# Three units of quarter products in the first matrix product of each token group instead of two, with their weight sums kept in DRAM

## The chip, the cores and the metric

The kernel runs on one core of a Trainium2 chip. Its engines are PE (TensorE: matmuls, with a weight load for each), DVE (VectorE), ACT (ScalarE), POOL (GpSimd) and SP (SyncE, which here only issues DMAs); each has its own queue and works it off in order. The metric is the device time of one execution in microseconds, as the median of several runs. One execution is also recorded by the hardware profiler; all durations below come from that one.

## The reference, cut to what matters

```python
# attention: q, k, v are (8, 8, 576, 64), fp32
scores = np.matmul(q, k.transpose(0, 1, 3, 2)) / 8
thresh = np.max(scores, axis=-1, keepdims=True) - tau
scores = np.where(scores >= thresh, scores, -1e9)
attn = np.exp(scores - np.max(scores, axis=-1, keepdims=True))
attn = attn / (attn.sum(axis=-1, keepdims=True) + 1e-9)
x = merge_heads(np.matmul(attn, v))            # (8, 576, 512)
# feed-forward: w_ch1 is (512, 2048), w_ch2 is (2048, 512)
mu, var = x.mean(-1), x.var(-1)
xn = (x - mu) / np.sqrt(var + 1e-6) * g_ln
out = x + np.maximum(xn @ w_ch1, 0) @ w_ch2
```

## The kernel before, in words

**Slots and groups.** The attention part runs over 72 slots, 9 per batch element (slot n belongs to element b = n // 9, with s = n % 9). A slot handles four blocks of 128 queries against 576 keys. The feed-forward part runs over 16 groups of 288 tokens, two per element. Its matmuls are poured into the slots by a generator (`ffn_steps`), step by step, as quotas allow (`second_part`, `dealt`, `owed`); the order on each engine is the order of issue. A group becomes ready some slots after its attention: an even group starts in the slot with s = 7, an odd group in the slot with s = 2 of the next element. Each of these groups fills about four and a half slots.

**One slot.** PE computes the scores (L434) into two PSUM tiles, `sc[0]` and `sc[1]`, three banks each. DVE reduces them to row maxima (`neg`, L450), POOL forms the threshold (`thr`, L454), ACT takes the exponentials (L463) into the room `e`, DVE masks and sums them (L473), POOL divides by the sums (L490), DVE transposes blocks of 32 (L559), SP writes the result to DRAM (`scr`, L580) and reads it back in the next slot as `em` and `er` (L594, L599). PE multiplies by the values one slot later (L638, and L649 at the end of the slot, into a corner of the score tiles). There is one room `e`: the exponentials of a slot overwrite it and so wait for the write of the slot before. In slots with s = 8, 0, 1, 2 DVE also transposes the next pair's q and k (`turn`, L368 to L378) between `neg` and the masking, after POOL has scaled q (L350); SP then loads the pair after that (L120).

**First part of a group.** hidden = relu(w_ch1 x), 16 chunks of 128 hidden features by 288 tokens. A plain chunk is 4 products (each two matmuls of 64 columns of weights, `product`, L103) over 288 tokens. A *unit* computes four chunks at once by a scheme of seven quarter products of 144 tokens instead of eight, with sums of weights and of x: one running PSUM tile `chain`, one tile `p2`, two regions in `sc[0]`, four additions on DVE (L940) and six ACT operations (L934 to L974). `chain`, `p2`, a plain chunk's `p1` and the segments of the second part share two PSUM banks (`ps_ff`), each free again when it has been copied out. The first unit of a group writes `chain` twice before the score tile; a later one writes `chain`, `p2` and then `sc[0]`, which must by then have been masked:

```python
order = (p5, p6, p3, p7) if k else (p6, p5, p7, p3)
```

Groups 0 and 1 are all plain. From group 2 on, two units are used, chunks 0 to 3 and 12 to 15, in two following slots; chunks 4 to 11 are plain.

**The sums of w_ch1.** While group 1 runs its second part (slots 13 to 15), `sums_of_w1` forms the weight sums: for each unit four steps, each three operations of 128x128 on DVE and one on POOL. One of the four is written over w_ch1 itself; the others, 12 pieces of 128x128 a unit, stay in SBUF: 21 in `extra`, two at the end of the room `e1`, one in the place of `ident`.

**Second part of a group.** Seven segments of quarter products of w_ch2 (`segment`), each 32 matmuls of 144 columns, with four sums of `hidden` formed in place (t3, t2, t4, t1, L1125, by_fours: two operations of 128x576 each). Those are queued in `drops` and issued by `drip`, or by `need` when due. b11 and b12 are the early and late tokens of chunks 0 to 7, b21 and b22 those of chunks 8 to 15. Segments in order: b11 (y11), b21, b12 after t3 = b22 - b12, b11 after t2 = b11 + t3 (y12), b21 after t4, b11 after t1, b22.

**Tail.** After slot 71 the last two groups run without attention beside them.

Of the kernel before, what the change touches and what calls it, by code (L numbers as in the profile page):

```python
# [18 lines left out]
def kernel(  # L19
# [824 lines left out]
                    eng.tensor_tensor(out=out[at], in0=a[at], in1=b[at], op=op)  # L844
                    yield

    UNITS = (((0, 1), (2, 3)), ((12, 13), (14, 15)))
    PLAIN = [d for d in range(ND) if all(d not in t for u in UNITS for t in u)]
    sums_due = []
    last_added = set()  # L850
# [2 lines left out]
        n, i = divmod(ready(g), QUARTERS)  # L853
        return [n + (i > 0) + k for k in range(len(UNITS))]

    def piece_of(k, which, c, m):


        i = ((k * 3 + which) * 2 + c) * 2 + m
        if i < 21:  # L860
            return extra[:, i]
        if i < 23:
            at = NB * 128 - 256 + (i - 21) * 128
            return flat(e_room[1])[:, at : at + 128]
        return ident

    def sums_of_w1():


        for k, (f1, f2) in enumerate(UNITS):  # L870
            for c in range(2):
                for m in range(2):
                    cols = [slice(128 * t[m], 128 * t[m] + 128) for t in (f1, f2)]
                    a11, a12 = (w1_sb[2 * j + c][:, cols[0]] for j in range(2))
                    a21, a22 = (w1_sb[2 * j + c][:, cols[1]] for j in range(2))
                    p2, p3, p4 = (piece_of(k, i, c, m) for i in range(3))
                    for eng, out, a, b, op in (
                        (nc.vector, p3, a11, a21, ALU.subtract),
                        (nc.vector, a21, a21, a22, ALU.add),
                        (nc.vector, p2, a21, a11, ALU.subtract),  # L880
                        (nc.gpsimd, p4, a12, p2, ALU.subtract),
                    ):
                        eng.tensor_tensor(out=out, in0=a, in1=b, op=op)
                    yield

    sums_of_x = {}

# [18 lines left out]
    def unit(g, xc, k):  # L906


        f1, f2 = UNITS[k]
        t1, t2, t3, t4 = sums_of_x[g]  # L910
        of = lambda f, j: hidden[:, f[0] : f[0] + 2, (early, late)[j]]
        h11, h12, h21, h22 = of(f1, 0), of(f1, 1), of(f2, 0), of(f2, 1)
        w_of = lambda f, j: lambda c, m: w1_sb[2 * j + c][:, 128 * f[m] : 128 * f[m] + 128]
        s_of = lambda which: lambda c, m: piece_of(k, which, c, m)
        x_of = lambda i, j: lambda c: xc[:, 2 * i + c, (early, late)[j]]
        t_of = lambda t: lambda c: t[:, c]
        other = [
            sc[0][:, 512 * i : 512 * i + TOK].rearrange("p (m t) -> p m t", m=2) for i in range(2)
        ]

        def steps(bank, lhs, rhs, first, last):
            for c in range(2):
                for m in range(2):
                    product(
                        bank[:, m], lhsT=lhs(c, m), rhs=rhs(c),
                        start=first and c == m == 0, stop=last and c == m == 1,
                        skip_group_check=True,
                    )
                    yield c == m == 1

        chain = ps_ff.tile([128, 2, HT], F32, tag="ff", name="chain")
        for _ in steps(chain, w_of(f1, 0), x_of(0, 0), True, False):
            yield 3, 0.5
        nc.scalar.copy(h12, chain)  # L934
        p2 = ps_ff.tile([128, 2, HT], F32, tag="ff", name="p2")
        for _ in steps(p2, w_of(f1, 1), x_of(1, 0), True, True):
            yield 3, 0.5

        def add(out, a, b):
            ins = nc.vector.tensor_tensor(out=out, in0=a, in1=b, op=ALU.add)  # L940
            if any(a is t for t in other):
                other_reads.append(ins.ins)

        def after_p6():
            nc.scalar.copy(h22, chain)
            sums_due.append(lambda: add(h12, other[0], h22))

        def after_p7():
            nc.scalar.copy(h21, chain)
            sums_due.append(lambda: add(h22, other[0], h21))  # L950

        sums_due.append(lambda: add(h11, p2, h12))
        p5 = steps(other[0], w_of(f2, 0), t_of(t1), True, True), lambda: None
        p6 = steps(chain, s_of(0), t_of(t2), False, False), after_p6
        p7 = steps(chain, s_of(1), t_of(t3), False, False), after_p7
        p3 = (
            steps(other[1], s_of(2), x_of(1, 1), True, True),
            lambda: sums_due.append(lambda: add(h12, other[1], h12)),
        )
        order = (p5, p6, p3, p7) if k else (p6, p5, p7, p3)  # L960
        for i, (part_of, after) in enumerate(order):
            for end in part_of:
                if end:
                    after()
                stop = end and now < QUARTERS * NS and (i == 3 or i == 0 and part < 2)
                yield 4 if stop else 3, 0.5
        for end in steps(chain, w_of(f2, 1), t_of(t4), False, True):
            if not end:
                yield 3, 0.5
        run_all(sums_due)  # L970
        nc.scalar.activation(h21, chain, func=AF.Relu)
        both = hidden[:, f1[0] : f1[0] + 2]
        nc.scalar.activation(both, both, func=AF.Relu)
        nc.scalar.activation(h22, h22, func=AF.Relu)  # L974
        yield 2 if k else 3, 0.5
# [10 lines left out]
    def add_squares(sq, *which):  # L986
        for c in which:
            nc.gpsimd.tensor_tensor(out=sq[:, 0], in0=sq[:, 0], in1=sq[:, c], op=ALU.add)  # L988

    def first_units(g):  # L990


        xc = centred[g]
        plain, slots = PLAIN[:], unit_slots(g)
        sq = hidden[:, ND - NK :]
        k = 0
        due = False
        while plain or k < len(UNITS):
            if k < len(UNITS) and (not plain or now // QUARTERS >= slots[k] and part > 1):
                yield from unit(g, xc, k)  # L1000
                k += 1
                if k == 1:
                    due = plain and owed >= 1
                    if not due:
                        bank = ps_ff.tile([128, HT], F32, tag="ff", name="var")
                        rb = variance(g, average(spare[g], bank, sq[:, 0], True, eps_sb))
                        yield 2, 0.5
                continue
            d = plain.pop(0)
            bank = ps_ff.tile([128, 512], F32, tag="ff", name="p1")  # L1010
            p1 = bank[:, :TOK]
            for c in range(NK):
                if due and c == NK - 1:
                    spread = average(spare[g], bank[:, TOK : TOK + HT], sq[:, 0], False, eps_sb)
                    yield 1, 0.5
                product(
                    p1, lhsT=w1_sb[c][:, d * 128 : (d + 1) * 128], rhs=xc[:, c],
                    start=(c == 0), stop=(c == NK - 1),
                )
                if c < NK - 1:  # L1020
                    yield 1, 1
            nc.scalar.activation(hidden[:, d], p1, func=AF.Relu)  # L1022
            if due:
                due = False
                rb = variance(g, spread)
            yield 2, 1
        sums_of_x.pop(g)
        return rb

    def first_part(g):  # L1030
# [64 lines left out]
    def second_quarters(g, rb):  # L1095
# [83 lines left out]

        dve, pool = nc.vector, nc.gpsimd  # L1180
        ends_here = g == NG - 1
        later(("t3", 3, by_fours, pool, b12, b22, b12, ALU.subtract), urgent=pool)
        banks_taken[0] = True
        yield from segment(w2[0, 0], b11, y11)
        need("t3")
        later(("t2", 3, by_fours, dve, b11, b11, b12, ALU.add), urgent=dve)
        yield 2, 0.5
        p2 = yield from segment(w2[0, 1], b21)
        need("t2")
        later(("t4", 3, by_fours, pool, b21, b21, b11, ALU.subtract), urgent=pool)  # L1190
# [42 lines left out]
    def ffn_steps(g):  # L1233
        rb = yield from (first_part if g < 2 else first_units)(g)
        sums = sums_of_w1() if g == 1 else iter(())
        for i, step in enumerate((second_quarters if g else second_plain)(g, rb)):
            if i % 13 == 12:
                next(sums, None)
            yield step

# [31 lines left out]
    def second_part(n, i):  # L1272
# [13 lines left out]
        else:  # L1286
            if i == 0:
                share = remain / (ready(g + 1) // QUARTERS - n)
                if has_unit:
                    first = [(share - UNIT_COST) * r / sum(ROOM[:2]) for r in ROOM[:2]]  # L1290
                    dealt[:] = [*first, UNIT_COST - 2, 2]
                else:
                    dealt[:] = [share * r / sum(ROOM) for r in ROOM]
            owed += dealt[i]
# [4 lines left out]
        steps = 0  # L1299
        whole = i in (0, QUARTERS - 1) or i == 1 and has_unit  # L1300
        got = 1 if i in (0, QUARTERS - 1) else 3 if i == 2 and has_unit else 2
        least = 2 if has_unit and i < 2 else 0.5
        while queue and (owed >= least or got == 3 or got == 1 and whole):
            got, cost = next(queue[0], (None, 0))
            if got is None:
# [228 lines left out]
```

## Time and profile before

| | |
|---|---|
| Median of 3 runs | 1316.91 us (1315.94 to 1317.62) |
| The profiled execution's own time | 1317.26 us |
| Its span | 1315.4 us |
| PE busy | 1280.6 us |
| DVE / POOL / ACT busy | 948.3 / 638.2 / 515.0 us |
| Granted TensorE clock | 0.997 |
| DMA | 214.11 MB, mean 163 GB/s |
| Share of SP's DMA queue, of 16 engines | 54.8% |

In a timeline, each line is a group of like instructions: start and duration in us, engine, line of the kernel, operation, output <- inputs, shape, number of records, and in brackets the idle time of the engine before it with what ended it. The table of waits gives, for a waiting instruction and the one that released it, the total in us, the number of times and the longest. "+8.03" in the text means 8.03 us after the first score matmul of that slot. Slots quoted: slot 38 starts at 640.68, 39 at 657.91, 44 at 739.08, 45 at 757.92 and 46 at 774.38 us.

### The profile page before, as it was taken

Reading aid. Unit: us, or ns where it says so; the run is one execution under the profiler, and the core shown is the slowest. Engines: PE = TensorE matmul, PEld = TensorE weight load, DVE = VectorE, ACT = ScalarE, POOL = GpSimd, SP = SyncE. Lnnn points to the kernel's source line nnn. Section 1 sums busy time; section 2 is a strip of 40 time slices with the busy share of each in tenths; the row PEclk is TensorE's granted clock in tenths of the full one; section 3 lists DMA queues with packets and bytes.
Section 4 is the critical chain, followed back from the end, with each engine's and each line's share of the span. In section 5 each row is a group of like instructions: output and inputs, shape, how many; then the busy total and the mean of one; then the engine's idle time right before and its main releaser. Section 6 shows DMA issues by size and latency. Waiting matters only on the chain.

```text
span 1315.4 us, 43423 instructions
## 1 busy us (share of the span) xinstructions
PE 1280.6 (97%) x18648; PEld 1050.7 (80%) x18648; DVE 948.3 (72%) x1722; ACT 515.0 (39%) x1163; POOL 638.2 (49%) x858
## 2 busy tenths in 40 slices
PE   8899889999999999999999999999999999999997
PEld 7665556879788887978879897888878788798977
DVE  7879878976777587776868777775877768687223
ACT  5866343343433434242343424334342423434130
POOL 3465565545445354544535454453545445354413
PEclk9999999999999999999999999999999999999999
DMA  8937865466644675546744566446764457453111
GB/s 154 295 112 185 205 171 193 151 173 171 191 164 163 170 205 168 166 159 155 216 154 158 172 169 192 163 163 171 190 191 157 160 146 202 157 168 140 52 19 19
DMA packets 335311, 214.11 MB, mean 163 GB/s; under 512 B 247376, under 2 KB 292688, under 8 KB 327056
## 3 DMA queue, kind: packets, MB, share of 16 engines
q1 hardware_dynamic: 329008, 210.46, 54.8%
q8 instruction: 146, 2.39, 0.7%
q10 hardware_dynamic: 5952, 0.74, 0.4%
q14 instruction: 45, 0.37, 0.1%
q0 software_dynamic: 160, 0.15, 0.1%
HBM read 124.00 MB, written 87.29 MB: 161 GB/s over the span
## 4 chain that ended last, share of the span: by engine, by line
PE 74%; DVE 3%; POOL 1%; DMA 1%; ACT 1%; issue 1%; POOLq 0%; DVEq 0%; ACTq 0%
PE seg L103 28%; PE p L103 16%; PE chain L103 8%; PE sc L434 8%; PE sc L638 7%; PE sc L103 4%; PE sc L649 2%; DVE e L473 1%; DMA scr<-e 1%; DVE neg L450 1%; POOL sum L692 0%; DVE e L559 0%; POOL thr L454 0%; PE mean L708 0%; POOL e L490 0%
## 5 line engine op out<-in xcount | busy, mean ns | idle before, releaser
L103 PE MATMUL p<-xc,w 128*64 128x288 f32 (+1 forms) x2752 | 327.9, 389 | 4.9 <-ACT hidden L1022 2.9
L450 DVE TENSOR_REDUCE neg<-sc 128x2 f32<-128x1152 f32 x144 | 189.5, 1353 | 144.7 <-PE sc L434 142.6
L103 PEld LDWEIGHTS p<-xc,w 128*64 128x64 f32 x2752 | 188.0, 137 | 123.9 <-issue 11.2
L490 POOL TENSOR_SCALAR e<-e,den 128x576 f32<-128x576 f32 x264 | 205.4, 791 | 95.2 <-DVE den L478 94.9
L103 PE MATMUL seg<-hidden,w 128*64 128x144 f32 x3840 | 244.0, 287 | 0.0
L103 PEld LDWEIGHTS seg<-hidden,w 128*64 128x64 f32 x3840 | 234.8, 137 | 9.3 <-issue 7.9
L473 DVE SCALAR_TENSOR_TENSOR e<-sc,thr,e 128x576 f32<-128x576 f32 x288 | 222.3, 809 | 15.6 <-POOL thr L454 8.6
L454 POOL TENSOR_SCALAR thr<-neg,low_sb 128x2 f32<-128x2 f32 x144 | 45.4, 316 | 335.8 <-DVE neg L450 334.5
L463 ACT ACTIVATE e<-sc,neg 128x576 f32<-128x576 f32 x288 | 196.5, 752 | 17.3 <-DMA scr<-e 13.5
L559 DVE STREAM_TRANSPOSE e<-e 128x1152 f32<-128x1152 f32 (+1 forms) x113 | 163.8, 1451 | 22.7 <-POOL e L490 22.0
L434 PE MATMUL sc<-kT,qT 64*64 64x384 f32 (+3 forms) x2048 | 139.4, 403 | 1.6 <-DVE e L473 1.6
L638 PE MATMUL sc<-em,v_in 128*64 128x128 f32 (+1 forms) x2368 | 130.6, 264 | 3.7 <-DVE e L473 2.0
L638 PEld LDWEIGHTS sc<-em,v_in 128*64 128x64 f32 x2368 | 122.3, 138 | 7.1 <-DVE e L473 3.0
L103 PE MATMUL seg<-hidden,stage 128*64 128x144 f32 x1920 | 124.3, 286 | 0.6 <-ACT y L1140 0.6
L103 PEld LDWEIGHTS seg<-hidden,stage 128*64 128x64 f32 x1920 | 117.4, 137 | 3.6 <-issue 2.5
L434 PEld LDWEIGHTS sc<-kT,qT 64*64 64x64 f32 x2048 | 76.0, 133 | 42.6 <-issue 21.3
L1140 ACT COPY part<-seg 128x288 f32<-128x288 f32 x74 | 29.9, 404 | 181.3 <-PE seg L103 152.9
L1125 POOL TENSOR_TENSOR hidden<-hidden 128x576 f32<-128x576 f32 x60 | 84.2, 1423 | 30.0 <-ACT hidden L1022 16.8
L663 ACT COPY x<-sc 128x128 f32<-128x128 f32 x120 | 31.2, 265 | 164.8 <-PE sc L434 109.1
L1125 DVE TENSOR_TENSOR hidden<-hidden 128x576 f32<-128x576 f32 x60 | 52.6, 905 | 41.7 <-PE seg L103 35.8
L988 POOL TENSOR_TENSOR hidden<-hidden 128x288 f32<-128x288 f32 x48 | 39.0, 812 | 77.9 <-ACT hidden L1335 76.4
L1022 ACT ACTIVATE hidden<-p 128x288 f32<-128x288 f32 x112 | 47.2, 422 | 56.0 <-PE p L103 55.9
(163 smaller groups left out, 1633.9 us busy)
## 6 DMA issues: line engine op xcount, KB each, us to landing
scr<-e SPq DMA_DIRECT2D x60, 1152.0 KB, 5.0
em<-scr SPq DMA_DIRECT2D x63, 1024.0 KB, 5.7
out_dram<-ot SPq DMA_DIRECT2D x248, 36.0 KB, 3.7
q_in<-in_q_dram SPq DMA_DIRECT2D x120, 72.0 KB, 2.6
er<-scr SPq DMA_DIRECT2D x132, 64.0 KB, 5.1
k_in<-in_k_dram SPq DMA_DIRECT2D x116, 72.0 KB, 2.9
v_in<-in_v_dram SPq DMA_DIRECT2D x28, 256.0 KB, 5.5
w<-in_moe_w_ch_dram SPq DMA_DIRECT2D x10, 512.0 KB, 8.6
```

The source lines that it names most:

```text
L103: nc.tensor.matmul(out[r], lhsT=lhsT[:, r], rhs=rhs, **flags)
L434: mm = nc.tensor.matmul(sc[h][64 * i : 64 * i + 64, at : at + n], lhsT=ql[r] if s == HP else qT[r, half, j * 128 + 64 * i : j * 128 + 64 * ...
L450: nc.vector.tensor_reduce(out=neg[:, i], in_=pairs[h], axis=AXL.X, op=ALU.max, negate=True,)
L454: nc.gpsimd.tensor_scalar(out=thr[:, i], in0=neg[:, i], scalar1=-1.0, scalar2=low_sb, op0=ALU.mult, op1=ALU.add,)
L463: nc.scalar.activation(blocks_of(es, i, n), like(blocks[i], n), func=AF.Exp, bias=neg[:, i : i + 1])
L473: nc.vector.scalar_tensor_tensor(out=e, in0=like(blocks[i], n), scalar=thr[:, i : i + 1], in1=e, op0=ALU.is_ge, op1=ALU.mult, accum_out=de ...
L490: nc.gpsimd.tensor_scalar(out=e, in0=e, scalar1=den[:, i : i + 1], scalar2=1.0, op0=ALU.mult, op1=ALU.mult,)
L559: nc.vector.transpose(et[:, :, at], et[:, :, at])
L638: mm = nc.tensor.matmul(dst[64 * h : 64 * h + 64], lhsT=vt[:, h, c, :], rhs=pick(em[:, 2 * j : 2 * j + 2, c], h), start=c == 0 and first, ...
L988: nc.gpsimd.tensor_tensor(out=sq[:, 0], in0=sq[:, 0], in1=sq[:, c], op=ALU.add)
L1022: nc.scalar.activation(hidden[:, d], p1, func=AF.Relu)
L1125: eng.tensor_tensor(out=out[at], in0=in0[at], in1=in1[at], op=op)
```

## The change

A third unit takes chunks 4 to 7; chunks 8 to 11 remain plain. The twelve pieces of each unit's sums are stored to DRAM (`sums0` to `sums2`, 768 KB each). In SBUF there are two rooms of twelve pieces: 12 of `extra`, and the other 9 of `extra` with the end of `e1` and the place of `ident`. Units use the rooms in turn (`room_for`); when a unit has been issued, the sums of the unit after next are loaded into its room on SP, at quarter 1 of the slot after (`unit_and_load`, `load_sums`). The third unit runs inside the second part, between the segment y11 and the segment on b21; a slot with one of the first two units has two plain chunks ahead of it. From group 2 on, t3 and t2 are issued after the third unit, and both run on POOL. The third unit's sums pass through tiles of the pool `o` on their way to DRAM. The steps of `sums_of_w1` come every 9 steps instead of every 13, twelve of them.

```diff
-    UNITS = (((0, 1), (2, 3)), ((12, 13), (14, 15)))
+    UNITS = (((0, 1), (2, 3)), ((4, 5), (6, 7)), ((12, 13), (14, 15)))
...
+    PIECES = 12
+    stored = [
+        dram.tile([128, PIECES, 128], F32, tag=f"sums{k}", bufs=1, name=f"sums{k}")
+        for k in range(len(UNITS))
+    ]
+    def rooms_of(room):
+        if room == 0:
+            return [(0, extra[:, :PIECES])]
+        end = flat(e_room[1])[:, NB * 128 - 256 : NB * 128]
+        return [
+            (0, extra[:, PIECES:21]),
+            (9, end.rearrange("p (i c) -> p i c", c=128)),
+            (11, ident.rearrange("p (i c) -> p i c", i=1)),
+        ]
+    def room_for(g, k):
+        return (len(UNITS) * g + k) % 2
+    def store_sums(k):
+        for at, pieces in rooms_of(room_for(2, k)):
+            nc.sync.dma_start(out=stored[k][:, at : at + pieces.shape[1]], in_=pieces)
+    def load_sums(g, k):
+        for at, pieces in rooms_of(room_for(g, k)):
+            nc.sync.dma_start(out=pieces, in_=stored[k][:, at : at + pieces.shape[1]])
...
     def sums_of_w1():
...
-                    p2, p3, p4 = (piece_of(k, i, c, m) for i in range(3))
+                    if k < 2:
+                        p2, p3, p4 = (piece_of(room_for(2, k), i, c, m) for i in range(3))
+                    else:
+                        two = [ffn.tile([128, TOK], F32, tag="o", bufs=4, name="sum") for _ in range(2)]
+                        p2, p3, p4 = two[0][:, :128], two[0][:, 128:256], two[1][:, :128]
...
+                    for i, piece in enumerate((p2, p3, p4) if k == 2 else ()):
+                        nc.sync.dma_start(out=stored[k][:, (i * 2 + c) * 2 + m], in_=piece)
                     yield
+            if k < 2:
+                store_sums(k)
...
+    def second_half(g, k):
+        n = unit_slots(g)[k]
+        while now < QUARTERS * min(NS, n + 1) and (now < QUARTERS * n or part < 2):
+            yield 0, 0
+    def unit_and_load(g, k):
+        yield from second_half(g, k)
+        n = max(now // QUARTERS, unit_slots(g)[k])
+        yield from unit(g, centred[g], k)
+        h, i = divmod(len(UNITS) * g + k + 2, len(UNITS))
+        if h < NG:
+            at_quarter(max(n, now // QUARTERS) + 1, 1, load_sums, h, i)
     def first_units(g):
...
+        for k in range(2):
+            for d in PLAIN[2 * k : 2 * k + 2]:
...
+            yield from unit_and_load(g, k)
...
-        later(("t3", 3, by_fours, pool, b12, b22, b12, ALU.subtract), urgent=pool)
-        banks_taken[0] = True
+        t3 = "t3", 3, by_fours, pool, b12, b22, b12, ALU.subtract
+        t2 = "t2", 3, by_fours, dve if g == 1 else pool, b11, b11, b12, ALU.add
+        if g == 1:
+            later(t3, urgent=pool)
+            banks_taken[0] = True
         yield from segment(w2[0, 0], b11, y11)
-        need("t3")
-        later(("t2", 3, by_fours, dve, b11, b11, b12, ALU.add), urgent=dve)
+        if g == 1:
+            need("t3")
+            later(t2, urgent=dve)
         yield 2, 0.5
+        if g > 1:
+            yield from unit_and_load(g, 2)
+            sums_of_x.pop(g)
+            later(t3, t2, urgent=pool)
+            banks_taken[0] = True
         p2 = yield from segment(w2[0, 1], b21)
...
-            if i % 13 == 12:
+            if i % 9 == 8:
                 next(sums, None)
...
-                if has_unit:
-                    first = [(share - UNIT_COST) * r / sum(ROOM[:2]) for r in ROOM[:2]]
-                    dealt[:] = [*first, UNIT_COST - 2, 2]
+                if has_unit and n < unit_slots(g)[2]:
+                    dealt[:] = [4, 4, UNIT_COST - 2, 2]
+                elif has_unit:
+                    dealt[:] = [3, 5, UNIT_COST - 2, max(2, share - 6 - UNIT_COST)]
...
-        least = 2 if has_unit and i < 2 else 0.5
+        least = 2 if has_unit and i < 2 and n < unit_slots(g)[2] else 0.5
```

More of the change, by code (lines that the diff above doesn't have):

```diff
@@ L854, in unit_slots, with piece_of @@
         return [n + (i > 0) + k for k in range(len(UNITS))]
[L856 to L865, printed above, removed]
+    PIECES = 12
[12 more added lines that the diff above has]
+        ]
+    def piece_of(room, which, c, m):
+        i = (which * 2 + c) * 2 + m
+        at, pieces = [r for r in rooms_of(room) if r[0] <= i][-1]
+        return pieces[:, i - at]
+    def room_for(g, k):
[6 more added lines that the diff above has]
+            nc.sync.dma_start(out=pieces, in_=stored[k][:, at : at + pieces.shape[1]])
     def sums_of_w1():
@@ L913, in unit @@
         w_of = lambda f, j: lambda c, m: w1_sb[2 * j + c][:, 128 * f[m] : 128 * f[m] + 128]
-        s_of = lambda which: lambda c, m: piece_of(k, which, c, m)
+        s_of = lambda which: lambda c, m: piece_of(room_for(g, k), which, c, m)
         x_of = lambda i, j: lambda c: xc[:, 2 * i + c, (early, late)[j]]
@@ L990, in first_units @@
     def first_units(g):
         xc = centred[g]
-        plain, slots = PLAIN[:], unit_slots(g)
         sq = hidden[:, ND - NK :]
-        k = 0
         due = False
[L998 to L1026, printed above, removed]
@@ L1027, in first_units @@
-        sums_of_x.pop(g)
+        for k in range(2):
+            for d in PLAIN[2 * k : 2 * k + 2]:
+                bank = ps_ff.tile([128, 512], F32, tag="ff", name="p1")
+                p1 = bank[:, :TOK]
+                for c in range(NK):
+                    if due and c == NK - 1:
+                        spread = average(spare[g], bank[:, TOK : TOK + HT], sq[:, 0], False, eps_sb)
+                        yield 1, 0.5
+                    product(
+                        p1, lhsT=w1_sb[c][:, d * 128 : (d + 1) * 128], rhs=xc[:, c],
+                        start=(c == 0), stop=(c == NK - 1),
+                    )
+                    if c < NK - 1:
+                        yield 1, 1
+                nc.scalar.activation(hidden[:, d], p1, func=AF.Relu)
+                if due:
+                    due = False
+                    rb = variance(g, spread)
+                yield 2, 1
+            yield from unit_and_load(g, k)
+            if k == 0:
+                due = now >= QUARTERS * NS
+                if not due:
+                    bank = ps_ff.tile([128, HT], F32, tag="ff", name="var")
+                    rb = variance(g, average(spare[g], bank, sq[:, 0], True, eps_sb))
+                    yield 2, 0.5
```

## The prediction

> **What bounds the kernel now.** I read the page first: its span, then the busy shares.
>
> ```profile
> span 1315.4 us, 43423 instructions
> PE 1280.6 (97%) x18648; PEld 1050.7 (80%) x18648; DVE 948.3 (72%) x1722; ACT 515.0 (39%) x1163; POOL 638.2 (49%) x858
> ```
>
> PE is the bound, with 34.8 us of idle time in the whole span. The second view, the waits of PE alone between 220 and 1180 us (columns: total us, times, longest), shows that almost none of that idle time lies in the periodic part:
>
> ```profile
> PE p L103 <- ACT hidden L1022: 2.9, 7, 1.4
> PE sc L103 <- DVE e L473: 0.9, 6, 0.2
> PE seg L103 <- ACT y L1140: 0.6, 2, 0.4
> ```
>
> So a microsecond taken from PE is a microsecond gained as long as no new wait arises, and every new wait of PE is lost in full. The third view is the timeline of PE in slots 43 and 44 (start, duration, instruction group). Each matmul of the program leaves two records here.
>
> ```profile
> 722.05 7.98 PE L103 MATMUL p<-xc,w 128*64 128x288 f32 x64
> 729.86 1.15 PE L103 MATMUL chain<-xc,w 128*64 128x144 f32 x16
> ...
> 735.74 1.92 PE L638 MATMUL sc<-em,v_in 128*64 128x128 f32 x32
> 737.49 1.15 PE L103 MATMUL chain<-t,w 128*64 128x144 f32 x16
> 738.47 0.41 PE L708 MATMUL var<-hidden,avg_sb 128*64 128x144 f32 x4
> ```
>
> Four plain chunks of the first part (64 records of 288 columns) last from 722.05 to 729.86, 7.81 us. A unit (112 records of 144 columns) lasts from 729.86 to 738.47 without the values from 735.74 to 737.49, 6.86 us. A record of 144 columns costs 61 ns and one of 288 costs 122 ns: halving the columns halves the time.
>
> **Term 1, the matmuls.** Chunks 4 to 7 go from plain to a unit in each of 14 groups: 14 x (7.81 - 6.86) = **-13.3 us**. The built program agrees in count: 9,662 matmuls instead of 9,326, which is 14 x (56 - 32) more, of half the width. [...]
>
> **Term 2, waits that go.** In slot 39 (an odd group's second unit behind a single plain chunk) the timeline has PE idle for 0.25 us before p2 (an eviction on ACT queued behind exponentials) and 0.15 us before the first product into the score banks. With two plain chunks ahead, as in slot 38, neither shows. Six groups (3, 5, ... 13): 6 x 0.40 = **-2.4 us**. The 1.4 us in the table is slot 16 and belongs to term 4.
>
> **Term 3, waits that come in the even groups.** Units now begin behind two chunks, 5.98 us after the slot's scores begin (slot 38: 640.68 to 646.66). For the second and third unit the first product into the score banks comes third, 2 x 1.02 us later, at +8.03. It must wait until DVE has masked both blocks of sc0. In slot 44 DVE turns the next pair's q and k first:
>
> ```profile
> 741.24 2.82 DVE L450 TENSOR_REDUCE neg<-sc 128x2 f32<-128x1152 f32 x2 [2.38 <-PE sc L434]
> 743.97 0.77 DVE L368 STREAM_TRANSPOSE kT<-k_in 128x576 f32<-128x576 f32 x1
> 745.19 0.77 DVE L372 STREAM_TRANSPOSE qT<-q_in 128x256 f32<-128x256 f32 x2 [0.45 <-POOL q_in L350]
> ...
> 747.45 0.08 DVE L473 DVE_READ_ACCUMULATOR e<-sc,thr,e 128x1 f32 x1
> ```
>
> Scores began at 739.08, the second block ends at 747.53 (+8.45), and a release takes 0.05 (slot 39: 664.65 to 664.70): PE waits 8.50 - 8.03 = 0.47 us. Before, the unit stood behind three chunks and waited for nothing. In slot 45, now also a unit's slot with a turn, t3 no longer stands ahead of the scaling of q on POOL, so slot 46's row holds (turn done at +6.74), then two blocks of together 1.53 us (slot 38), +0.05: +8.32, 0.29 us of wait.
> Slot 45 has a second candidate. The sums of the third unit (768 KB) are loaded on SP behind slot 44's q and k (issued until +11.7) and ahead of that slot's write of weights (issued at +13.3, landed at +18.7 by the next fetch's issue, 757.82). Slot 44 becomes 18.84 - 3.9 + 0.47 = 15.4 us long, so the landing, +3.3 in slot 45, lies 0.4 us ahead of the exponentials (+3.71) that overwrite the same room. The load adds between nothing and 2.0 us (768 KB at about 390 GB/s: the windows give 412 and 370 in the two microseconds from 740). Behind the exponentials, on ACT, stands the copy of y11 that frees p2's bank; it ended at +6.64 against +7.0 needed, 0.36 us of cover. So slot 45 costs 0.3 to 1.25 us; I take 0.5, because q's and k's small packets still fill the engines while the load starts and only part of it falls on the write. Per group about 1.0, in the six even groups 2 to 12 (group 14 has no turn): **+6 us**, bounds 4.6 and 10.3. Odd groups stay clear: their turn falls on the first unit (needed at +9.0, ready at +8.3), their other two slots have no turn (ready at +6.75).
>
> **Term 4, the start.** The sums of w_ch1 grow from 8 steps to 12 (two subtractions and an addition on DVE, one subtraction on POOL each), still within slots 13 to 15, where DVE has no idle time left from 229.55 until 265.2:
>
> ```profile
> 229.55 2.62 DVE L450 TENSOR_REDUCE neg<-sc 128x2 f32<-128x1152 f32 x2 [0.95 <-PE sc L434]
> ...
> 262.59 2.61 DVE L450 TENSOR_REDUCE neg<-sc 128x2 f32<-128x1152 f32 x2
> 265.60 0.82 DVE L473 SCALAR_TENSOR_TENSOR e<-sc,thr,e 128x576 f32<-128x576 f32 x1 [0.40 <-POOL thr L454]
> ```
>
> The 8 steps took 11.7 us of the DVE timeline, 1.46 each (0.86 where POOL rests, 1.7 or more where it works). Four more are 5.8 us; 0.95 of idle time takes its part, so slot 16's neg comes 4.9 us later. That slot's evictions, behind the exponentials, already cost PE 1.42 us; now p2 starts at 267.43 + 4.9 and ends at 273.3, where before the same work, two chunks (3.9 us) less than at 271.76, was done at 267.85. Loss **+5.5 us**. Bounds 3.1 (0.86 a step) and 7.1 (1.6 a step, and 1 us for the third unit's sums, whose tiles are reused only when their stores have landed: DVE waits there, and the weights' transposes, xc and neg are queued behind it).
>
> **Term 5, the tail.** Without attention between them, the last two chain stretches of a unit wait for the copy (0.50 us before 1279.90, in the last group's second unit). One such unit becomes three, and a plain eviction behind the variance can cost 0.5; the 0.46 and 0.18 us of waits around the old variance go: **+0.9 us**, 0.4 to 1.4.
>
> **At nothing**, with the cover: t2 moves from DVE to POOL (1.423 us instead of 0.905, 28 instructions, 40 us of POOL): it is due one segment of 3.9 us after t3, and it ends about 5.9 us after the unit, ahead of y12's segment at 7.8. In slot 41 it holds thr back by 1.4 us; the values that need those weights come 2 us after them. If that cover went, 1 us in 7 groups. DVE keeps its sum: four additions a unit (1.8 us) for two t2 (1.8 us). ACT gets six operations of 2.72 us for four of 1.69; it is 39% busy, and the order of evictions that could hurt is in term 3. The other loads land a slot or more ahead of use; 33 MB beside 214 MB lie on queues at 55%.
>
> **Sum.** -13.3 - 2.4 + 6.0 + 5.5 + 0.9 = -3.3 us on the profiled execution's own 1317.26 us: 1314.0. That execution stands 0.35 above the median of 1316.91: **1313.6 us**. With the bounds: -7.6 to +3.1, so 1309.3 to 1320.0.
>
> **Rivals.** (a) The waits don't come: DVE's extra steps find POOL at rest and the score banks are ready; only 3.1 of the start and 2 of term 3 stay. -13.3 - 2.4 + 5.1 + 0.4 = -10.2, about 1306.7. Against it: the rows above are already at their limit. Chance 0.15.
> (b) Slower: the loads in front of the weights' write. One mechanism, in slot 45 of six groups: if the 768 KB move nearer to the page's mean of 163 GB/s (4.8 us) than to 390, the write lands about 3 us later, at +6.3, the exponentials start 2.6 us late, and PE waits 2.2 us for p2's bank instead of 0.5: 6 x 1.7 = 10 us more, about 1324. It decides from a landing at +4.3 in slot 45, where the gain is gone (0.55 us more, six times). For it: the write already delays exponentials in the waits of ACT (13.5 us, 11 times between 220 and 1180 us). Against it: the engines moved 412 GB/s in the microsecond from 740. Chance 0.2.
> (c) The change does not do what it says: excluded by the counts of the built program; the order of PE shows all three units in every group from 2 on. Chance below 0.01.
>
> **How the numbers follow.** The forecast has 0.65. A measurement of this kernel can tell about 0.2%, 2.6 us, from no change: faster means below 1314.3, slower above 1319.5. The forecast's own range lies with 0.6 of its chance below 1314.3 and with 0.05 above 1319.5. Faster: 0.39 + 0.15 = 0.54. Slower: 0.2 + 0.03 = 0.23. Same: 0.23. The range reaches into both rivals: 1306 to 1322.5.
>
> **What would show it.** Right: matmuls p of 288 columns from 2304 records to 1408; PE waiting for DVE e L473 about 0.5 us in slot 44 and again in slot 45; slot 16's neg about 5 us later than 262.59; slot 40 at 15.3 us instead of 13.7. Wrong: PE waits in slots 38 to 42, a wait of PE for the loaded sums, exponentials waiting for the write by over 1 us in slot 45, or units longer than 6.9 us.

## The result, and the profile after

The changed kernel takes 1337.57 us (median of 4 runs, 1331.73 to 1338.7); the kernel before takes 1317.26 us (4 runs, 1315.94 to 1318.7). The ratio is 1.0145, 95% interval 1.0114 to 1.0176. The forecast was 1313.6 us, with a range of 1306 to 1322.5: wrong in sign and outside the range.

The head of the page of the changed kernel:

```profile
span 1336.1 us, 45057 instructions
PE 1280.0 (96%) x19320; PEld 1090.4 (82%) x19320; DVE 961.8 (72%) x1762; ACT 528.6 (40%) x1191; POOL 674.2 (50%) x890
...
PE 66%; DMA 4%; DVE 3%; ACT 2%; POOL 2%; issue 2%; POOLq 0%; ACTq 0%; DVEq 0%; SPq 0%
```

PE's busy time should have fallen by 13.3 us and fell by 0.6; the span grew by 20.7. Part of the missing fall is matmuls at half speed (below), which count as busy: with the load moved (first experiment) PE is busy for 1275.1 us. The last line is the chain that ended last: DMA holds 4% of the path (before: 1%), nearly all of it the write of the weights.

The waits of PE between 220 and 1180 us (total us, times, longest), 4.4 us before:

```profile
PE p L103 <- ACT y L1181: 13.9, 6, 3.1
PE chain L103 <- ACT hidden L1057: 2.6, 1, 2.6
PE p L103 <- DVE xc L742: 2.4, 1, 2.4
PE sc L638 <- DVE e L473: 2.2, 3, 1.3
PE sc L103 <- DVE e L473: 1.9, 6, 0.3
```

The first line is one wait in each of the six even groups: the third unit's p2 waits for the bank that y11's copy frees. The next three lines are the start (slots 14 to 16). The last line is the wait for the masked score bank that the prediction put at 0.29 and 0.47 us.

Where the 20.7 us lie follows from the starts of the slots in the two traces. The row on the start counts slots 14 to 16 against a slot 16 that is 3.78 us shorter, as the first unit's slot is in every other even group (15.30 instead of 19.08 us).

| Part of the run | Predicted | Measured |
|---|---|---|
| Slots 0 to 13 | 0 | +0.6 |
| Start, slots 14 to 16 | +5.5 | +9.6 |
| Six even groups (2 to 12) | 6 x (-0.95 + 1.0) = +0.3 | +20.7 |
| Six odd groups (3 to 13) | 6 x (-0.95 - 0.40) = -8.1 | -10.1 |
| Slot 70 and the tail, groups 14 and 15 | 2 x -0.95 + 0.9 = -1.0 | -0.2 |
| Sum (of the rounded rows) | -3.3 | +20.6 |

The 20.7 us of the even groups lie almost wholly in one slot of each, the slot of the third unit (18, 27, 36, 45, 54, 63). With the load moved (first experiment below) this slot lasts 21.51 us; here it lasts 23.43, 21.72, 25.55, 26.15, 25.68 and 25.90, together 19.4 us more. Slot 45, which starts at 763.28, on three engines. SP from slot 44 on, ACT, and then PE:

```profile
760.13 0.62 SPq L891 DMA_DIRECT2D extra<-sums  x1
761.02 0.36 SPq L580 DMA_DIRECT2D scr<-e  x1
...
770.58 0.38 SPq L594 DMA_DIRECT2D em<-scr  x1
```

```profile
770.61 2.64 ACT L463 ACTIVATE e<-sc,neg 128x576 f32<-128x576 f32 x4 [3.51 <-DMA scr<-e]
773.12 0.42 ACT L1181 COPY y<-seg 128x288 f32<-128x288 f32 x1
```

```profile
769.30 1.15 PE L103 MATMUL chain<-xc,w 128*64 128x144 f32 x16
773.58 1.96 PE L103 MATMUL p<-xc,w 128*64 128x144 f32 x16 [3.13 <-ACT y L1181]
775.33 2.11 PE L103 MATMUL sc<-t,w 128*64 128x144 f32 x16
777.25 1.17 PE L103 MATMUL chain<-t,extra 128*64 128x144 f32 x16
```

The same places in the kernel before (SP in slot 44, ACT in slot 45, which starts at 757.92):

```profile
752.40 0.36 SPq L580 DMA_DIRECT2D scr<-e  x1
...
757.82 0.38 SPq L594 DMA_DIRECT2D em<-scr  x1
```

```profile
761.63 2.64 ACT L463 ACTIVATE e<-sc,neg 128x576 f32<-128x576 f32 x4
764.16 0.40 ACT L1140 COPY y<-seg 128x288 f32<-128x288 f32 x1
```

The third unit's sums are loaded 0.9 us ahead of the write. The fetch that waits for the write goes out 9.56 us after it (5.42 in the same slot before), at +7.30 of slot 45. The exponentials that overwrite the room start at +7.33 instead of +3.71. Behind them on ACT stands y11's copy (773.12, though its segment had ended at 769.47), and behind that PE's p2: 3.13 us of wait. This is one of the prediction's own signs of being wrong: the exponentials wait 3.51 us for the write, and 1 us was its limit. Then PE pays a second time: 16 records of 144 columns take 1.96 and 2.11 us instead of 1.15 to 1.20. This is the granted clock: 0.91 in the 20 us from 760, where the kernel before has 1.00 in every such stretch from 160 to 1300 us.

### The profile page after: what moved, and what is told of

The parts are those of the page before. It is cut to its first block, busy times and chain, and to the rows that moved or that the text cites. A ratio compares the mean times of both kernels' runs of the same rounds, so it can differ in the third digit from the quotient of the medians.

```text
span 1336.1 us, 45057 instructions
## 1 busy us (share of the span) xinstructions
PE 1280.0 (96%) x19320; PEld 1090.4 (82%) x19320; DVE 961.8 (72%) x1762; ACT 528.6 (40%) x1191; POOL 674.2 (50%) x890
## 4 chain that ended last, share of the span: by engine, by line
PE 66%; DMA 4%; DVE 3%; ACT 2%; POOL 2%; issue 2%; POOLq 0%; ACTq 0%; DVEq 0%; SPq 0%
PE seg L103 27%; PE chain L103 10%; PE p L103 8%; PE sc L434 7%; PE sc L638 7%; PE sc L103 5%; DMA scr<-e 4%; DVE e L473 2%; ACT e L463 1%; PE sc L649 1%; DVE neg L450 1%; POOL e L490 1%; DMA v_in<-in_v_dram 1%; POOL q_in L350 0%; POOL sum L692 0%
## 5 line engine op out<-in xcount | busy, mean ns | idle before, releaser
L103 PE MATMUL p<-xc,w 128*64 128x288 f32 (+1 forms) x2080 | 233.4, 374 | 18.8 <-ACT y L1181 13.9
L103 PEld LDWEIGHTS p<-xc,w 128*64 128x64 f32 x2080 | 139.4, 138 | 100.2 <-ACT y L1181 15.5
L463 ACT ACTIVATE e<-sc,neg 128x576 f32<-128x576 f32 x288 | 196.4, 754 | 22.2 <-DMA scr<-e 17.9
L1166 POOL TENSOR_TENSOR hidden<-hidden 128x576 f32<-128x576 f32 x88 | 122.6, 1419 | 97.4 <-ACT hidden L1008 88.6
L454 POOL TENSOR_SCALAR thr<-neg,low_sb 128x2 f32<-128x2 f32 x144 | 39.7, 276 | 252.8 <-DVE neg L450 250.8
L103 PE MATMUL chain<-t,extra 128*64 128x144 f32 x1344 | 99.2, 291 | 0.0
L103 PEld LDWEIGHTS chain<-t,extra 128*64 128x64 f32 x1344 | 86.8, 140 | 0.0
```

Of the source, the lines that this page charges most:

```text
L103: nc.tensor.matmul(out[r], lhsT=lhsT[:, r], rhs=rhs, **flags)
L454: nc.gpsimd.tensor_scalar(out=thr[:, i], in0=neg[:, i], scalar1=-1.0, scalar2=low_sb, op0=ALU.mult, op1=ALU.add,)
L463: nc.scalar.activation(blocks_of(es, i, n), like(blocks[i], n), func=AF.Exp, bias=neg[:, i : i + 1])
L1166: eng.tensor_tensor(out=out[at], in0=in0[at], in1=in1[at], op=op)
```

## The experiments

All times are medians, beside runs of the kernel before on the same chip (1318.2 to 1318.7 us in these series). Theory A: the 768 KB load ahead of the weights' write, in a slot 44 that has become 3.2 us shorter, is the loss of the even groups. Rivals: the shorter slot alone (theory B); the 31 MB of extra traffic as such (theory C); the order on SP alone.

**The load behind the write.**

```diff
-            at_quarter(max(n, now // QUARTERS) + 1, 1, load_sums, h, i)
+            at = 3 if k == 0 and g % 2 == 0 else 1
+            at_quarter(max(n, now // QUARTERS) + 1, at, load_sums, h, i)
```

> The 768 KB load of the third unit's sums in the even groups is issued on SP behind the weights' write of the same slot instead of ahead of it; nothing else changes. Theory A (the load ahead of the write is the whole loss): the write lands 5 to 6 us after its issue instead of 9.5, the exponentials of slot 45 wait under 1 us, slot 45 lasts 21.1 to 21.7 us instead of 26.15, and the sum over the six even groups, 20.4 us, is gone: 1317 us, 1315 to 1319. Theory B (slot 44 is 3.2 us shorter than before, so the next exponentials come too early for any write): PE still waits over 1.5 us in slot 45 and the time stays above 1328.

1319.17 us (10 runs); ratio to before 1.0008 (0.9998 to 1.0019) instead of 1.0145: about 18 us are back. The same place in the trace, slot 45 starting at 759.52, and the line of ACT's waits between 220 and 1180 us (17.9 us in 8 before the edit):

```profile
757.25 0.36 SPq L580 DMA_DIRECT2D scr<-e  x1
757.65 0.43 SPq L891 DMA_DIRECT2D extra<-sums  x1
...
764.06 0.38 SPq L594 DMA_DIRECT2D em<-scr  x1
```

```profile
ACT e L463 <- DMA scr<-e: 3.1, 4, 1.3
```

The write is issued at the same place, +13.31 of slot 44, and has landed 6.81 us later, the worst of the six. Five third-unit slots last 21.50 or 21.51 us, this one 21.72. The load itself is still there and still arrives in time. The shorter slot alone is therefore not the cause.

**No loads of sums at all.**

```diff
-            at_quarter(max(n, now // QUARTERS) + 1, 1, load_sums, h, i)
+            pass
```

> All loads of stored sums are left out, so units 2 and 3 multiply by whatever lies in their room (the output is not the reference's; the work of PE, DVE, ACT and POOL is the same). Theory A: as with the load behind the write, 1315 to 1317.5, within 2 us of it. Theory C (31 MB more of transfers cost something in every slot): well below that run, 1305 to 1312.

1318.24 us (10 runs), ratio 0.9997 (0.9988 to 1.0006). That is 0.9 us less than with the load behind the write, no more than the scatter of the runs. The loads elsewhere, and the traffic as such, cost about a microsecond at most: theory C falls. Nor does PE's table of waits in the changed kernel show any wait for loaded sums.

**Half of the load ahead.**

```diff
+            if k == 0 and g % 2 == 0:
+                at_quarter(n, 1, load_half, h, i, 0)
+                at_quarter(n, 3, load_half, h, i, 1)
```

> Half of that load (384 KB) stays ahead of the weights' write, the other half goes behind it. Theory A, if the delay goes by bytes: the write lands 7 to 7.5 us after its issue, PE waits about 1 us in slot 45, too short to lower the clock; slot 45 lasts 22 to 23 us, the time is 1320 to 1327. If a transfer ahead of the write costs by its place and not by its bytes, 1333 or more.

1321.24 us (6 runs), ratio 1.0029 (1.0017 to 1.0041). PE waits 0.74 us in slot 36 and 1.14 in slot 45, nothing in the other four. That a wait of about 1 us would leave the clock up was the author's estimate; the changed kernel's trace has waits of 0.38 us (slot 27) and 2.09 us (slot 18) with the granted clock at 1.00 after both. On average the delay grows faster than the bytes, as the table below shows: the mean goes from 5.7 to 6.6 to 8.7 us for 0, 384 and 768 KB ahead, though single slots overlap.

**The kernel before with the same load ahead.** The first unit's sums are read once more from DRAM, in the even groups' second slot, between k and the write.

```diff
+    def load_again():
+        nc.sync.dma_start(out=extra[:, :12], in_=stored)
...
+                if k == 0 and g % 2 == 0:
+                    at_quarter(max(now // QUARTERS, slots[0]) + 1, 1, load_again)
```

> The kernel before with one more load: after the even groups' first unit its 768 KB of sums are read again from DRAM into the same room, issued on SP in slot 44 between the k load and the weights' write, where the third unit's load stood. Theory A with the shorter slot: the load delays the write by 3 to 4 us here too, but slot 44 is 18.84 us long, so the write (issued at +13.3, landed some 9 us later, +3.5 to +4 of slot 45) meets the exponentials at +3.7 and costs PE nothing or a few tenths: 1317 to 1320. If a load ahead of the write costs by itself, whatever the slot's length: 1325 to 1340.

1317.86 us (10 runs), ratio 0.9996 (0.9985 to 1.0006): no loss. The slowest of its writes, in slot 35 (SP, then ACT in slot 36, which starts at 606.50):

```profile
600.38 0.62 SPq L870 DMA_DIRECT2D extra<-sums  x1
601.10 0.36 SPq L580 DMA_DIRECT2D scr<-e  x1
610.79 0.38 SPq L594 DMA_DIRECT2D em<-scr  x1
```

```profile
610.82 2.64 ACT L463 ACTIVATE e<-sc,neg 128x576 f32<-128x576 f32 x4 [0.51 <-DMA scr<-e]
613.33 0.42 ACT L1149 COPY y<-seg 128x288 f32<-128x288 f32 x1
```

This write is as late as in the changed kernel, 9.69 us after its issue, but the slot is 18.84 us long: it lands at +4.29 instead of +7.30. y11's copy ends at 613.75, +7.25, and PE, which has two segments (8.06 us) behind its scores here, asks for that bank only at 616.44, +9.94. In the changed kernel the third unit asks at 770.45, +7.17. So the load was harmless alone, and the shorter slot was harmless alone; together with the earlier need for the bank they cost 19 us. That the earlier need has a part is worked out from the times, not run: here a request at +7.17 would have waited 0.1 us, and in the changed kernel, where y11's copy ends at +10.26, a request at +9.94 would have waited 0.3 us instead of 3.13.

**The load ahead, but early.** Quarter 0 of slot 44 instead of 1.

```diff
+            at = 0 if k == 0 and g % 2 == 0 else 1
+            at_quarter(max(n, now // QUARTERS) + 1, at, load_sums, h, i)
```

> The changed kernel with the even groups' third load issued early in slot 44 (behind the fetch of the turned weights, ahead of the stores and the loads of q and k, some 8 us earlier than in the changed kernel), so it still stands ahead of the weights' write on SP. Theory A (the two transfers share the engines when they are in flight together): the load has landed before the write is issued at +13.3, the write lands within 5 to 7 us, slot 45 lasts 21.5 us: 1317 to 1321. If it is the order on SP that delays the write: as the changed kernel, above 1330.

1319.43 us (10 runs), ratio 1.0002 (0.9987 to 1.0016). The load is still ahead of the write on SP, and the write lands in 5.2 to 6.4 us. So the order on SP alone did not delay it. Nor did a load in flight beside it: in the first experiment the load goes out 0.4 us after the write, and the write still lands in 5.7 us on average. The write was late where all of the load stood ahead of it with its bytes still to move (issued 0.7 to 1.6 us earlier in the changed kernel): 8.7 us on average there, 8.5 in the kernel before with the same load. One slot of six lost 1.6 us, where the write itself was issued at +15.17: it stands on SP behind the loads of q and k, and the last q load went out at +12.09 (+9.24 in the changed kernel). SP's waits between 740 and 757 us put 1.9 us on the fetch `em` and 0.3 on the early load.

From the issue of the write to the issue of the fetch that waits for it, in us, in the six slots before the third unit's (the same slots in the kernel before):

| Kernel | 17 | 26 | 35 | 44 | 53 | 62 | mean |
|---|---|---|---|---|---|---|---|
| before | 5.38 | 5.11 | 5.18 | 5.42 | 6.74 | 5.79 | 5.6 |
| changed | 8.53 | 6.78 | 9.14 | 9.56 | 9.10 | 9.20 | 8.7 |
| load behind | 5.47 | 4.95 | 6.11 | 6.81 | 5.41 | 5.35 | 5.7 |
| no loads | 5.43 | 6.03 | 6.10 | 7.09 | 5.21 | 5.08 | 5.8 |
| half ahead | 6.04 | 6.13 | 7.18 | 7.58 | 6.40 | 6.27 | 6.6 |
| before, with load | 8.84 | 9.20 | 9.69 | 7.34 | 7.51 | 8.27 | 8.5 |
| load early | 5.58 | 5.18 | 5.72 | 6.36 | 5.33 | 5.33 | 5.6 |

**The start: wider operations.** Load behind the write; each pair of sums of w_ch1 (m = 0, 1) in one operation of 256 columns, half as many steps, every 18 instead of every 9.

```diff
-                for m in range(2):
-                    cols = [slice(128 * t[m], 128 * t[m] + 128) for t in (f1, f2)]
+                cols = [slice(128 * t[0], 128 * t[0] + 256) for t in (f1, f2)]
...
-            if i % 9 == 8:
+            if i % 18 == 17:
```

> Load behind the write, as in the first run, and the sums of w_ch1 in slots 13 to 15 made in operations of 256 columns instead of 128 (45 operations on DVE become 18 and some narrow ones). If DVE's work there is what the start costs (slots 14 to 16 are 5.8 us longer than before the change), 2 to 4 us come back: 1313 to 1315. If it is the stores of the third unit's sums that DVE waits for (1.8 us in the trace), nothing comes back: 1316 to 1318.

1311.59 us (4 runs), ratio 0.9955 (0.9938 to 0.9972): 7.6 us less than with narrow sums, twice what was expected. Slots 14 to 16 take 49.56 us; with narrow sums and the load behind they take 57.10, in the kernel before 51.62. DVE's time on the sums falls from 18.9 to 11.0 us, and PE's waits in slots 14 and 15 are gone. Some 1.5 us of the gain in these slots is the clock: with narrow sums it fell to half speed in slot 16 (from 278.25 us) and here it did not; in the last experiment, with the same wide sums, it fell there again, and slot 16 lasts 20.12 us instead of 18.61.

**The kernel before with the wide sums.** The same edit on two units.

> The kernel before with two units a group, its sums of w_ch1 made in operations of 256 columns, nothing else changed. It tells how much of the 6.6 us that the third unit with wide sums and the load behind the write gained belongs to the sums. If the third unit is what gains: 1315 to 1318 here. If the wide sums are most of it: 1311 to 1313.

1318.43 us (10 runs), ratio 0.9994 (0.9985 to 1.0003). The wide sums gain nothing by themselves: slots 14 to 16 take 51.36 us with them and 51.62 with the eight narrow steps. The 6.6 us by which the run above beats the kernel before belong to the third unit.

**The start: no small stores.** Narrow sums, load behind the write; one store in place of the third unit's twelve.

```diff
-                    for i, piece in enumerate((p2, p3, p4) if k == 2 else ()):
-                        nc.sync.dma_start(out=stored[k][:, (i * 2 + c) * 2 + m], in_=piece)
...
+            if k == 0:
+                nc.sync.dma_start(out=stored[2], in_=extra[:, :PIECES])
```

> Load behind the write, narrow sums, and the third unit's sums are computed but not stored piece by piece: one store of the first unit's sums takes the place of the twelve stores (the third unit multiplies by the wrong sums). If the stores, on which DVE waits 1.8 us before slot 16, carry the start's excess: slots 14 to 16 shorten by 2 us or more, 1315 to 1317. If DVE's narrow operations carry it: within 1 us of the 1319.2 of the kernel with the load behind the write.

1317.11 us (10 runs, 1315.68 to 1323.64), 2.1 us under the run with the stores, which ran on another chip and whose range (1316.81 to 1321.96) overlaps it; between the two expectations. The trace says more: slots 14 to 16 take 55.96 us instead of 57.10, and the waits for late masks in slot 14 stay. So the stores carry 1.1 of the 7.5 us that the wide sums removed and the clock some 1.5. The rest is put down to DVE's operations, as what is left over: the wide sums also halved the number of steps and stores.

**Own bank first.** Load behind the write, wide sums, and one order for all units.

```diff
-        order = (p5, p6, p3, p7) if k else (p6, p5, p7, p3)
+        order = p6, p5, p7, p3
```

> The third unit with wide sums and the load behind the write, and in all three units the product into the own bank first and the one into the score bank second, as the first unit has it. The waits of PE for the masked score bank (2.9 us in 11 places) go: 1308 to 1310 against 1311.6. If the copies of the chain bank, queued behind the exponentials on ACT, come later than the masks, that wait takes their place and nothing is gained: 1311 to 1314.

1305.71 us (4 runs, 1303.98 to 1306.0), ratio 0.990 (0.9885 to 0.9915): the best of all, 13 us under the kernel before. Its waits of PE between 220 and 1180 us:

```profile
PE chain L103 <- ACT hidden L1085: 2.6, 1, 2.6
PE p L103 <- ACT hidden L1085: 0.7, 2, 0.4
...
PE p L103 <- ACT y L1209: 0.2, 1, 0.2
```

The waits for the score bank are gone: the even groups' slots like 44 and 45 are 0.35 us shorter each than with the old order (15.22 us, and 21.17 in five of six). The stretch from slot 71 to the end is 2.1 us shorter too, which was not expected; 1.5 us of it are three waits of 0.5 us for the copy of `chain`, which the trace shows with the old order and not with the new.

## Why the prediction was wrong

**The step that failed is term 3, second candidate, the third unit's load.** It said that the load "adds between nothing and 2.0 us" to the write and that slot 45 costs 0.3 to 1.25 us. The load added 3.1 us on average (8.7 instead of 5.6), up to 4.1. It was priced as its own bytes at the rate of two microseconds in which no load of q or k was in flight. In the trace the write's bytes moved only when the load's were nearly through, and the load's only when k's were. In three stretches of slots 44 and 45 of the changed kernel (share of the DMA engines and GB/s in the last two columns):

```profile
757.50:762.50 5.00, 5.00 (x90) 5.00 (x88) 4.53 (x9) 0.80 (x2) 1.91 (x3) 1.00 0.82 107
762.50:768.70 6.20, 6.20 (x106) 5.03 (x104) 4.83 (x7) 1.85 (x5) 1.52 (x4) 1.00 0.96 342
768.70:770.40 1.70, 1.70 (x30) 1.48 (x26) 0.94 (x4) 0.00 (x0) 0.46 (x1) 1.00 0.17 53
```

While k's small packets move (the engines busy for 0.82 of the time) the rate is 107 GB/s, and the load, though issued at 760.13, has not started when the write is issued at 761.02. The packets of the trace can be told apart by size: those of 128 bytes, which come with the loads of q and k, end at 762.58, the load's (6144 bytes) run from 761.38 to 766.12, the write's (9216 bytes) only from 764.82 to 770.01. From 762.5 on, load, write and the values behind it (768 + 1152 + 320 KB) take 6.2 us at 342 GB/s. Then 1.7 us pass in which a sixth of the engines' time is busy, and only then has the write landed. With the load behind it (first experiment, same slot) the write's packets run from 758.14 to 762.25 and the load's from 761.75 to 765.43: the load lands 2.0 us after the write and costs it nothing that shows (landed 6.81 us after its issue, 7.09 in the run without loads). The prediction named the small packets, but as a reason for taking less.

**Rival (b) had the chain right, and its price was still too low.** It had the landing at +6.3 and a wait of 2.2 us; the exponentials started at +6.5 and PE waited 2.3 us on average. Missing was the clock, which the prediction priced nowhere: in the four slots with a wait of 2.67 to 3.13 us the slot grew by 1.3 to 1.5 us more than the wait, in the two with 0.38 and 2.09 it did not. That is the 5.5 us between 13.9 of wait and 19.4 of loss. The chance of 0.2 rested on "the engines moved 412 GB/s", a rate without loads of q and k beside it, and the cover of 0.36 us, which the text itself had worked out, left no room for an error of 3 us.

**Term 4, the start, was too small:** 9.6 us instead of 5.5, beyond the bound of 7.1. The twelve steps took DVE 18.9 us, 1.58 each, against 1.46 in the eight before; slot 16's `neg` came 8.1 us later, 0.6 of it older, and not 4.9. PE already lost in slots 14 and 15, where the values waited for late masks (the 2.2 us in the table of waits); the prediction looked at slot 16 alone. In slot 16 the clock fell too (half speed from 275.52 us). DVE in the changed kernel:

```profile
259.57 0.17 DVE L478 RECIPROCAL den<-den 128x2 f32<-128x2 f32 x1
261.55 0.29 DVE L913 TENSOR_TENSOR sum<-w 128x128 f32<-128x128 f32 x1 [1.81 <-DMA sums<-sum]
...
270.72 2.62 DVE L450 TENSOR_REDUCE neg<-sc 128x2 f32<-128x1152 f32 x2
```

The wait for the stores' tiles, bounded at 1 us, was 1.81.

**What held.** Term 1: 1408 records of 288 columns instead of 2304; in slot 43 two plain chunks take 3.93 us and a unit 6.96 (738.36 to 747.06 without the values), 0.1 above forecast. Term 2: the odd groups gained 1.7 us each, 1.35 forecast. Slot 40 lasts 15.24 us, 15.3 forecast. The waits for the score bank: 0.33 in slot 44, 0.47 forecast; with the load behind the write they show in five of the third unit's slots too, 0.16 each where 0.29 was forecast. Slot 70 and the tail were 0.8 us worse than forecast; why stays open.

## What to carry to other kernels

A transfer that something waits for was late by what stood ahead of it on its queue and had not moved yet (the write took 8.7 us on average with 768 KB ahead, 5.6 before the change); what stood behind it cost nothing that shows (5.7). Price a new one ahead of it by all the bytes still to move, at the rate of that stretch, and put it behind, or early enough to have landed. Small changes that each spend a margin (a shorter slot, an earlier need for a bank, a load) must be added up against that one margin before any of them is booked "at nothing". A wait of PE can cost more than itself: those of 2.67 to 3.13 us cost 1.3 to 1.5 us more here, and after two of 0.66 and 1.34 us close together PE ran at half speed too (the run with the early load, from 243.21); one of 2.09 us cost no more than itself.

## What the hardware showed that was not expected

**Half speed came on a grid of 3.413 us, and the length of a wait alone did not settle it.** After waits of 2.67 to 3.13 us PE ran at half speed (123 ns instead of 61 for a record of 144 columns) for one or two products, some 1.5 us each time. In the granted clock of the changed kernel half-speed stretches begin at 152.64, 275.52, 616.85, 773.86, 930.88, 1087.89 and 1333.65, the later six 36, 136, 182, 228, 274 and 346 times 3.413 us after the first; in the kernel before at 154.43 and 1311.54, 339 times 3.413 us apart. They last 3.41 to 6.83 us. So a run can be cut into windows of 3.413 us on that grid. The stretches in slots 36 and 45 of the changed kernel, each a window and the next one (PE's busy time comes first after the length, the granted clock stands third from the end):

```profile
613.44:616.85 3.41, 1.02 (x18) 0.75 (x14) 1.92 (x6) 2.67 (x5) 0.00 (x0) 1.00 0.48 83
616.85:620.26 3.41, 3.10 (x26) 3.06 (x28) 3.34 (x9) 0.56 (x2) 2.61 (x4) 0.50 1.11 322
770.45:773.86 3.41, 0.28 (x5) 0.28 (x6) 1.81 (x6) 3.23 (x6) 0.00 (x0) 1.00 0.52 194
773.86:777.27 3.41, 3.41 (x34) 3.41 (x32) 3.10 (x7) 0.00 (x0) 3.20 (x5) 0.50 0.95 229
```

The same wait in slot 16, 2.61 us in the run with the wide sums and 2.64 in the last experiment, falls differently on the windows: PE is idle for 0.54 and 0.33 of two windows in the first run, for 0.65 of one in the second. The clock stays up in the first run and falls in the second:

```profile
263.52:266.94 3.42, 1.58 (x14) 0.68 (x10) 3.39 (x5) 1.12 (x3) 2.63 (x4) 1.00 0.51 123
266.94:270.35 3.41, 2.28 (x34) 2.01 (x36) 2.98 (x9) 2.57 (x6) 2.85 (x6) 1.00 0.91 275
```

```profile
264.76:268.17 3.41, 1.20 (x16) 0.93 (x16) 3.01 (x5) 3.11 (x7) 3.15 (x6) 1.00 0.87 229
268.17:271.59 3.42, 3.07 (x26) 3.03 (x28) 3.21 (x9) 0.59 (x2) 2.85 (x5) 0.50 0.57 196
```

Of 753 windows at full speed in the traces of the two kernels (from 20 us on, each with a whole window after it), 8 were followed by half speed. In the 8 PE's records leave 0.62 to 0.93 of the window idle, 2.1 us or more; in the other 745 at most 0.59. The wait of 2.09 us in slot 18 (308.25 to 310.34) lay across two windows that meet at 309.65, idle for 0.41 and 0.20, and nothing fell; in the run with the early load two waits of 0.66 and 1.34 us, 2.00 us together between 239.84 and 242.18, or 0.59 of 3.413, were followed by half speed from 243.21. So no sharp limit shows.

**A load ahead of a write.** 768 KB issued 0.7 to 1.6 us ahead of a write of 1152 KB held it up by 3 us on average (1.7 to 4.1), 384 KB by 0.9. The same 768 KB issued about 10 us ahead of it (744.04 and 755.46 in slot 44 of that run), or 0.4 us behind it, held it up by nothing that shows (5.6 and 5.7 us on average from issue to landing, 5.6 in the kernel before).
